# Linear attention with a routed MLP on one core: diagonals shared with ScalarE, products cut in quarters, two chunks' states in one product

## The chip, the core and the metric

The kernel runs on one core of one Trainium2 chip. The metric is device time in microseconds for one launch. The core has five engines with queues of their own: TensorE (PE) multiplies matrices, VectorE (DVE) and GpSimd (POOL) work element by element, ScalarE (ACT) copies and applies functions, and SyncE (SP) starts most of the loads. An engine works through its queue in order; an instruction that waits for a semaphore holds up all behind it.

## The reference

Two blocks follow each other. The first is a linear attention with decay: for every batch (4), head (8) and channel a state of 48 x 48 runs over 768 tokens.

```python
for t in range(S):
    kt, vt, rt = (k[:, :, t], v[:, :, t], r[:, :, t])
    cur = np.einsum('bhd,bhe->bhde', u[None] * kt, vt)
    y[:, :, t] = np.einsum('bhd,bhde->bhe', rt, state + cur)
    state = w[None, :, :, None] * state + np.einsum('bhd,bhe->bhde', kt, vt)
```

Its output, with the heads side by side, is x of shape (4, 768, 384). The second block gives every token a score `x @ w_gate`, takes the 128 best tokens of each batch, and adds to these rows `sigmoid(score) * (relu(x @ w1) @ w2)`, with 1024 hidden channels. All data are float32.

## The kernel before

**Units.** The tokens are cut into units of 128; unit n is part n % 6 of batch n // 6, 24 in all. A unit consists of two chunks of 64 tokens, c = 0 and 1. The eight heads are four pairs hp of an even and an odd head (i = 0, 1); the even head of a pair stands on partitions 0 to 47, the odd one on 64 to 111. The recurrence becomes products of matrices:

- `scaled` (L239) multiplies the keys by a table of decays, on POOL.
- `bonus` (L243) and `bonus_scaled` (L249) form r*k and r*k*u on POOL; `bonus_sum` (L253, DVE) adds them up to `du`, one number per token and head. `diagonal` (L257, POOL) spreads `du` over a diagonal: `at`, 128 partitions x 8 heads x 64.
- `turn` (L266, L271) transposes keys and r on PE; ScalarE copies the keys to `kh` (L276), DVE multiplies r by a table into `rh` (L281).
- `products` (L288) is k^T v: for each pair and head one product over all 128 tokens, with 48 weight columns and 96 moving columns. The values lie in `vpad` in blocks, so that columns 0 to 47 belong to chunk 0 and 48 to 95 to chunk 1. The result goes to `rp` in PSUM.
- `scores` (L298) is k r^T for each chunk and head, `masked` (L303, DVE) puts the causal half of it over the diagonal in `at`.
- `added` (L309, DVE) adds the product of a chunk to the state before it. For chunk 0 this gives the state between the chunks; for chunk 1 it gives the state after the unit, which ScalarE scales by the decay (L316, `z`, four activations).
- `states` (L328) multiplies r with the state before each chunk, `values` (L344) multiplies `at` with the values. Both add up in two PSUM banks, y0 for even heads and y1 for odd ones. Between the two stands a `mark`: a tiny copy on ScalarE (L332) that waits for the last products of `states`, and for which the first product of `values` waits.
- `finish` (L361, L363) copies y0 and y1 to x on ScalarE in three copies; `stored` writes x to memory, `score` (L378, DVE) forms the router's scores.

**Order.** The order is written out by hand, unit by unit; nothing is rearranged. In unit n, PE does states(n-1), products(n), scores(n), values(n-1), turn(n+1). ScalarE does mark(n-1), the copies of y of unit n-1, kh(n+1), z(n+1), and `along` (below). DVE does added(n, 0), masked(n), added(n, 1), rh(n+1), du(n+1), score(n-1) and router work. POOL does scaled(n+2), diagonal(n+1), bonus(n+2). The loads of unit n+4 (k, r and two halves of v) are started by SP one by one, each behind a DVE instruction of unit n; the weights follow in eight parts from unit 6 on.

**Router and MLP.** Extra work is hung on places in the units by `step(n, where, ...)` and done by `work_at(n, where)`. From unit 2 on, `scores_along` (L388, L390) turns a column of scores into a row on PE and ScalarE, and `compare` (L398, L400) counts on DVE how many are higher. Three units after a batch's last one, `pick` (L448 on PE, L452 and L455 on DVE) yields the indices of the chosen tokens, and `fetch` (L464) starts an indirect gather from POOL. `chosen` (L480, L482) transposes the rows to `xt`; the MLP is eight parts `hidden` (L491) and eight `expert` (L500), spread over six units. Where the parts go is in two lists, `MOVE0` for batch 0 and `MOVE` for the others. The MLP of the last batch stands behind all units.

```python
MOVE0 = (-1, -1, 0, 0, 0, 0, 1, 1, 2, 2, 3, 3, 4, 4, 5, 5)
step(n + 5 - (b == 0), "turn" if b == 0 else "scores", chosen, b, z)
step(n + 5 + (MOVE if b else MOVE0)[i * 16 // len(parts)], "end", f, *a)
```

Of the kernel before, what the change touches and what calls it, by code (L numbers as in the profile page):

```python
# [7 lines left out]
F32 = mybir.dt.float32  # L8
# [9 lines left out]
def kernel(  # L18
# [23 lines left out]
    nc = tc.nc  # L42
# [50 lines left out]
    def load(n, part=None, behind=None):  # L93


        b, c = divmod(n, NC)
        rows = slice(c * T, (c + 1) * T)
        if part is None:
            for part in range(4):
                load(n, part)  # L100
            return
        if n >= NU:
            return
        if part == 0:
# [130 lines left out]

    KH, RH, RK, RKU, DU, AT, ZA, ZB, YP = ({} for _ in range(9))

    def scaled(n):
        nc.gpsimd.tensor_mul(kws[n % 3][:, :, :D], KIN[n], wk)  # L239

    def bonus(n):
        rk = RK[n] = work.tile([128, H, D], F32, name="rk")
        nc.gpsimd.tensor_mul(rk, rpads[n % NIN][:, :, :D], KIN[n])  # L243
        if n:
            bonus_scaled(n, nc.gpsimd)

    def bonus_scaled(n, engine):
        RKU[n] = work.tile([128, H, D], F32, name="rku")
        engine.tensor_mul(RKU[n], RK[n], ub)  # L249
# [4 lines left out]

    def diagonal(n):
        AT[n] = work.tile([128, H, C], F32, name="at", bufs=3)
        nc.gpsimd.tensor_mul(AT[n], dia[:, None, :].to_broadcast([128, H, C]),  # L257
                             DU[n].rearrange("t i p -> t (i p)")[:, :, None].to_broadcast([128, H, C]))

    def turn(n, keys=None, between=None):  # L260
        def two_heads(x, hp):
# [18 lines left out]
    def turned(n, pr):  # L280
        return nc.vector.tensor_mul(RH[n][:CH], pr[:CH], tr[:CH])  # L281

    def products(n):

        for hp in range(NP):
            for i in range(2):
                at = NP * C + hp % 2 * 2 * D
                nc.tensor.matmul(out=rp[i * PAD : i * PAD + D, hp // 2, at : at + 2 * D],  # L288
                                 lhsT=kws[n % 3][:, 2 * hp + i, :D], rhs=VIN[n][:, 2 * hp + i, :],
                                 start=True, stop=True)  # L290

    def scores(n):
        for hp in range(NP):
# [7 lines left out]
    def masked(n):  # L301
        at = AT[n].rearrange("s (i p) t -> s i p t", i=2)
        return nc.vector.copy_predicated(at, causal, rp[:, :, : NP * C].rearrange("s i (p t) -> s i p t", p=NP))  # L303

    def added(n, c):
        z = ZA[n] if c == 0 else ZB[n]
        g = work.tile([128, NP, D], F32, name=f"g{c}", bufs=3)
        sums = rp[:, :, NP * C : NP * (C + D)].rearrange("d b (p e) -> d b p e", p=2)
        op = nc.vector.tensor_add(g.rearrange("d (b p) e -> d b p e", p=2), sums[:, :, :, c * D : (c + 1) * D],  # L309
                                  z.rearrange("d (b p) e -> d b p e", p=2))  # L310
        if c == 0:
            ZB[n] = g
            return op
        ZA[n + 1] = work.tile([128, NP, D], F32, name="z", bufs=3)
        for hp in range(NP):
            nc.scalar.activation(ZA[n + 1][:, hp, :], g[:, hp, :], AF.Copy, scale=wc[:, hp : hp + 1])  # L316

    def states(n):


        YP[n] = [psum.tile([128, 512], F32, name=x) for x in ("y0", "y1")]
        for hp in range(NP):
            for j in range(2):
                for i in range(2):
                    rows = slice(i * PAD, i * PAD + D)
                    c = j ^ i
                    z = ZA[n] if c == 0 else ZB[n]
                    mm = nc.tensor.matmul(out=YP[n][i][j * C : (j + 1) * C, hp * D : (hp + 1) * D],  # L328
                                          lhsT=RH[n][rows, hp, c * C : (c + 1) * C], rhs=z[rows, hp, :],
                                          start=(hp == 0), stop=False, skip_group_check=True)  # L330
                    END[i, j] = mm
        behind = nc.scalar.copy(mark, tr[:1, 0, :1])  # L332
        for mm in END.values():
            tc.add_manual_dep(behind.ins, mm.ins.name, wait_for, reason="a mark behind the states' part")
        return behind

    def values(n, behind):

        for hp in range(NP):
            for i in range(2):  # L340
                for j in range(2):
                    c = j ^ i
                    ts = slice(c * C, (c + 1) * C)
                    mm = nc.tensor.matmul(out=YP[n][i][j * C : (j + 1) * C, hp * D : (hp + 1) * D],  # L344
                                          lhsT=AT[n][ts, i * NP + hp, :],
                                          rhs=VIN[n][ts, 2 * hp + i, c * D : (c + 1) * D],
                                          start=False, stop=(hp == NP - 1), skip_group_check=True)
                    if hp == 0 and i == 0 and j == 0:
                        tc.add_manual_dep(mm.ins, behind.ins.name, wait_for,
                                          reason="y's banks: the other row half is done")  # L350
# [5 lines left out]
    def finish(n):  # L356
        b, c = divmod(n, NC)
        x = xa[b][:, c, :]
        to = x.rearrange("t (p i d) -> t i p d", p=NP, i=2)
        y = [YP[n][i][:, : NP * D].rearrange("t (p d) -> t p d", p=NP) for i in range(2)]  # L360
        nc.scalar.copy(to[:, 0], y[0])  # L361
        for j in range(2):
            nc.scalar.copy(to[(1 - j) * C : (2 - j) * C, 1], y[1][j * C : (j + 1) * C])  # L363

# [157 lines left out]

    fill = {}

    def step(n, where, f, *a):
        fill.setdefault((n, where), []).append((f, a))
# [5 lines left out]
            yield expert, (b, z, f)  # L534


    MOVE0 = (-1, -1, 0, 0, 0, 0, 1, 1, 2, 2, 3, 3, 4, 4, 5, 5)
    MOVE = (0, 0, 0, 0, 1, 1, 2, 2, 3, 3, 3, 4, 4, 4, 5, 5)

    def plan(b):  # L540
        n = (b + 1) * NC
        for j in range(NC):
            step(n - NC + j + 2, "turn", scores_along, b, j)
            step(n - NC + j + 2, "turn", compare, b, j)
        step(n + 1, "turn", count, b)
        step(n + 1, "turn", parts_of_scores, b)
        step(n + 2, "turn", rank, b)
        for z in range(NST):
            step(n + 2, "turn", match, b, z)
            step(n + 3, "scores", pick, b, z)  # L550
            step(n + 3, "scores", fetch, b, z)
            step(n + 5 - (b == 0), "turn" if b == 0 else "scores", chosen, b, z)
        parts = [p for z in range(NST) for p in mlp(b, z)]
        for i, (f, a) in enumerate(parts):
            step(n + 5 + (MOVE if b else MOVE0)[i * 16 // len(parts)], "end", f, *a)

    for b in range(B):
        plan(b)
# [1 line left out]
    def work_at(n, where):  # L560
        for f, a in fill.get((n, where), []):
            f(*a)
# [8 lines left out]
    nc.sync.dma_start(out=wg, in_=bass.AP(tensor=moe_w_gate.tensor, offset=moe_w_gate.offset, ap=[[0, 128], [1, Dm]]))  # L571
    load(3)
    turned(0, pr)
    bonus_scaled(0, nc.vector)
    bonus_sum(0)
    onward = const.tile([128, 128], F32)
# [1 line left out]
    ones = const.tile([128, 2], BF16)  # L578
    nc.vector.memset(ones[:, 0:1], 1.0)
    nc.vector.memset(ones[:, 1:2], 0.0)  # L580
    scaled(0)
    diagonal(0)
    scaled(1)
    bonus(1)
    for n in range(NU):
        if n == 2:
            late_tables()
        b, c = divmod(n, NC)
        if c == 0:
            ZA[n] = zt  # L590
        if n:
            behind = states(n - 1)
        products(n)
        scores(n)
        work_at(n, "scores")
        load(n + 4, 0, added(n, 0))
        op = masked(n)
        load(n + 4, 2, op)
        if n:
            values(n - 1, behind)  # L600
            finish(n - 1)
# [94 lines left out]
```

## Time and profile before

| | |
|---|---|
| median of 3 runs | 167.73 us (166.64 to 168.81) |
| profiled execution | 163.72 us |
| its span, first to last instruction | 161.9 us |
| busy: PE, DVE, ACT, POOL | 144.7, 111.3, 76.2, 117.5 us |
| granted TensorE clock | 1.00 |

The profiled execution is 1.8 us longer than its span, and 4.0 us shorter than the median of the runs. All stamps below are microseconds from the start of the span. A row of a timeline has start, duration, engine and line of the kernel, operation, output <- inputs, shapes and count; in brackets stands how long the engine sat idle before it, and what ended that. A float32 product shows as two matmul records, each with a weight load of its own. "issue" is idle time for which the profile finds no semaphore.

### The profile page before, as it was taken

How to read it: one execution, taken by the hardware profiler on the slowest of the kernel's cores; microseconds unless marked ns; L12 is line 12 of the kernel's file. 1: busy time of each engine (PE TensorE's matmuls, PEld its weight loads, DVE VectorE, ACT ScalarE, POOL GpSimd, SP SyncE). 2: the span in 40 equal slices, each digit the busy share in tenths (PEclk: the TensorE clock that was granted, in tenths of full speed). 3: DMA queues.
4: the chain of work that ended last, by engine and by line, in shares of the span. 5: the costliest groups of instructions: out<-in, count | busy, mean ns of one | idle time of the engine just before them, and what ended most of it. 6: DMA issues, size and time to landing. Idle time of an engine off the chain costs nothing.

```text
span 161.9 us, 7852 instructions
## 1 busy us (share of the span) xinstructions
PE 144.7 (89%) x3278; PEld 118.3 (73%) x3278; DVE 111.3 (69%) x352; ACT 76.2 (47%) x251; POOL 117.5 (73%) x156
## 2 busy tenths in 40 slices
PE   6969979678887959999999999999999999989970
PEld 2558858567776849999767879999696788748730
DVE  7856768899899975757999787488976956701010
ACT  6636655545454770555465444546606645102100
POOL 8699999999989999558899989688987421022002
PEclk9999999999999999999999999999999999999999
DMA  4998699999889989999999978786403112011001
GB/s 70 214 175 158 146 221 201 197 195 202 173 192 215 242 205 208 237 227 220 208 260 225 225 152 211 178 183 148 103 4 101 55 49 101 0 49 53 0 0 49
DMA packets 82659, 24.50 MB, mean 151 GB/s; under 512 B 76352, under 2 KB 82240, under 8 KB 82624
## 3 DMA queue, kind: packets, MB, share of 16 engines
q1 hardware_dynamic: 79888, 19.67, 57.4%
q10 hardware_dynamic: 2224, 2.75, 4.8%
q0 software_dynamic: 512, 1.57, 2.7%
q8 instruction: 26, 0.43, 1.1%
q14 instruction: 9, 0.07, 0.2%
HBM read 18.48 MB, written 5.51 MB: 148 GB/s over the span
## 4 chain that ended last, share of the span: by engine, by line
PE 59%; POOL 16%; issue 12%; DMA 6%; DVE 2%; ACT 1%; POOLq 1%; ACTq 0%
PE m L491 10%; PE rp L288 8%; PE m L500 7%; PE rp L298 6%; PE y L328 6%; PE m L266 6%; PE y L344 5%; PE m L271 4%; POOL kw L239 4%; POOL at L257 4%; POOL rk L243 4%; DMA kin<-in_k_dram 3%; DMA xr<-out_dram,idx 3%; POOL rku L249 3%; PE m L138 3%
## 5 line engine op out<-in xcount | busy, mean ns | idle before, releaser
L257 POOL TENSOR_TENSOR at<-dia,du 128x512 f32<-128x512 f32 x24 | 29.7, 1237 | 10.9 <-DVE du L253 10.9
L288 PE MATMUL rp<-vpad,kw 128*48 128x96 f32 x384 | 21.2, 251 | 4.5 <-issue 1.7
L249 POOL TENSOR_TENSOR rku<-rk,ub 128x384 f32<-128x384 f32 x23 | 23.1, 1005 | 1.8
L239 POOL TENSOR_TENSOR kw<-kin,wk 128x384 f32<-128x384 f32 x23 | 23.8, 1035 | 0.3 <-DMA kin<-in_k_dram 0.2
L491 PE MATMUL m<-xt,w 128*128 128x128 f32 x192 | 23.3, 277 | 0.5 <-ACT xt L482 0.5
L491 PEld LDWEIGHTS m<-xt,w 128*128 128x128 f32 x192 | 22.3, 192 | 1.3 <-ACT xt L482 1.2
L243 POOL TENSOR_TENSOR rk<-rpad,kin 128x384 f32<-128x384 f32 x23 | 23.0, 999 | 0.0
L500 PE MATMUL m<-w,ht 128*128 128x384 f32 x64 | 22.7, 490 | 0.1
L361 ACT COPY x<-y 128x192 f32<-128x192 f32 x24 | 7.6, 319 | 31.4 <-PE y L344 29.1
L316 ACT ACTIVATE z<-g,wp 128x48 f32<-128x48 f32 x80 | 20.2, 326 | 1.9 <-DVE g L309 1.8
L288 PEld LDWEIGHTS rp<-vpad,kw 128*48 128x48 f32 x384 | 16.3, 122 | 6.5 <-issue 3.0
L281 DVE TENSOR_TENSOR rh<-m,tables 112x512 f32<-112x512 f32 x24 | 16.5, 688 | 5.2 <-PE m L271 3.3
L328 PE MATMUL y<-g,rh 48*64 48x48 f32 x384 | 17.1, 223 | 2.6 <-issue 2.6
L303 DVE COPY_PREDICATED at<-mask,rp 128x512 f32<-128x512 uint32 x24 | 17.7, 736 | 2.4 <-POOL at L257 2.4
L378 DVE SCALAR_TENSOR_TENSOR scr<-x,wg 128x384 f32<-128x384 f32 x24 | 17.0, 707 | 1.8 <-ACT x L363 1.8
L328 PEld LDWEIGHTS y<-z,rh 48*64 48x64 f32 x320 | 12.2, 134 | 7.0 <-issue 4.7
L298 PE MATMUL rp<-rh,kh 48*64 48x64 f32 x768 | 16.7, 224 | 0.0
L400 DVE TENSOR_SCALAR_CACHE_REDUCE gt<-along,sc 128x128 bf16<-128x128 f32 (+5 forms) x24 | 16.2, 675 | 0.2 <-issue 0.2
L266 PE MATMUL m<-ident,kw 128*112 128x128 f32 x92 | 14.9, 285 | 1.1 <-POOL kw L239 1.1
L298 PEld LDWEIGHTS rp<-rh,kh 48*64 48x64 f32 x768 | 13.4, 134 | 3.2
L344 PE MATMUL y<-vpad,at 64*64 64x48 f32 x768 | 15.5, 218 | 0.2 <-ACT mark L332 0.2
L500 PEld LDWEIGHTS m<-w,ht 128*128 128x128 f32 x64 | 11.4, 191 | 5.9 <-ACT kh L276 0.3
(95 smaller groups left out, 251.3 us busy)
## 6 DMA issues: line engine op xcount, KB each, us to landing
rpad<-in_r_dram SPq DMA_DIRECT2D x24, 192.0 KB, 4.5
vpad<-in_v_dram SPq DMA_DIRECT2D x48, 96.0 KB, 4.4
kin<-in_k_dram SPq DMA_DIRECT2D x23, 192.0 KB, 4.1
w<-in_moe_w_dram SPq DMA_DIRECT2D x8, 384.0 KB, 5.5
out_dram<-x ACTq DMA_DIRECT2D x14, 192.0 KB, 3.9
out_dram<-x SPq DMA_DIRECT2D x10, 192.0 KB, 2.1
k<-in_k_dram SPq DMA_DIRECT2D x1, 192.0 KB
ub<-in_u_dram SPq DMA_DIRECT2D x1, 192.0 KB
```

What stands on the lines that cost most here:

```text
L239: nc.gpsimd.tensor_mul(kws[n % 3][:, :, :D], KIN[n], wk)
L243: nc.gpsimd.tensor_mul(rk, rpads[n % NIN][:, :, :D], KIN[n])
L249: engine.tensor_mul(RKU[n], RK[n], ub)
L257: nc.gpsimd.tensor_mul(AT[n], dia[:, None, :].to_broadcast([128, H, C]), DU[n].rearrange("t i p -> t (i p)")[:, :, None].to_broadcast([128 ...
L266: nc.tensor.transpose(pk[:CH, hp, :], two_heads(kws[n % 3] if keys is None else keys, hp), ident)
L288: nc.tensor.matmul(out=rp[i * PAD : i * PAD + D, hp // 2, at : at + 2 * D], lhsT=kws[n % 3][:, 2 * hp + i, :D], rhs=VIN[n][:, 2 * hp + i, ...
L298: nc.tensor.matmul(out=rp[ts, i, hp * C : (hp + 1) * C], lhsT=KH[n][rows, hp, ts], rhs=RH[n][rows, hp, ts], start=True, stop=True)
L316: nc.scalar.activation(ZA[n + 1][:, hp, :], g[:, hp, :], AF.Copy, scale=wc[:, hp : hp + 1])
L328: mm = nc.tensor.matmul(out=YP[n][i][j * C : (j + 1) * C, hp * D : (hp + 1) * D], lhsT=RH[n][rows, hp, c * C : (c + 1) * C], rhs=z[rows, h ...
L344: mm = nc.tensor.matmul(out=YP[n][i][j * C : (j + 1) * C, hp * D : (hp + 1) * D], lhsT=AT[n][ts, i * NP + hp, :], rhs=VIN[n][ts, 2 * hp + ...
L491: nc.tensor.matmul(out=ph[:, f % 4, :], lhsT=w1[:, d, f * 128 : (f + 1) * 128], rhs=XT[b, z][:, d, :], start=(d == 0), stop=(d == KD - 1))
L500: nc.tensor.matmul(out=pe[:, :Dm], lhsT=HT[b, z][:, f, :], rhs=w2[:, f, :], start=(f == 0), stop=(f == FB - 1))
```

## The change

1. `diagonal`: in units 1 to 10, POOL does four of the eight heads only; the others are four activations (copy with a scale from `du`) on ScalarE, behind z(n+1) in its queue. Unit 0 and units 11 to 23 stay on POOL.
2. `scaled(0)` moves from POOL to DVE.
3. For units 10, 16 and 22 `bonus_scaled` stands behind the gather of the unit before in POOL's queue, not ahead of it (`picking`).
4. `products` of units 15, 16, 17, 21, 22, 23 are cut in two by chunks (`quarters`): 64 tokens, 48 weight columns, 48 moving columns. There are 16 products instead of 8, chunk 0 in the first PSUM bank and chunk 1 in the second; `added` reads them there.
5. `states` of units 1 to 5 and 7 to 10 (`merged`): for even heads one product over all 128 tokens with both states side by side as 96 moving columns, instead of two of 64 tokens and 48 columns. Half of the result is not used. For this the two states of a unit share a tile (`states_of`), y0 gets 96 columns for each pair, and `finish` takes two copies of 64 partitions for even heads in these units, not one of 128.
6. In batch 0, `chosen` comes at the end of unit 10 (the router's transposes are ahead of it before and after), and the first two `hidden` parts come behind `states` in unit 11, not at the end of unit 10.

```diff
+    def scaled(n, engine=None):
+        (engine or nc.gpsimd).tensor_mul(kws[n % 3][:, :, :D], KIN[n], wk)
...
-        if n:
+        if n and not picking(n - 1):
             bonus_scaled(n, nc.gpsimd)
+    def picking(n):
+        return n % NC == 3 and n > NC
...
     def diagonal(n):
         AT[n] = work.tile([128, H, C], F32, name="at", bufs=3)
-        nc.gpsimd.tensor_mul(AT[n], dia[:, None, :].to_broadcast([128, H, C]),
-                             DU[n].rearrange("t i p -> t (i p)")[:, :, None].to_broadcast([128, H, C]))
+        du = DU[n].rearrange("t i p -> t (i p)")
+        own = H // 2 if 0 < n < 2 * NC - 1 else 0
+        nc.gpsimd.tensor_mul(AT[n][:, own:, :], dia[:, None, :].to_broadcast([128, H - own, C]),
+                             du[:, own:, None].to_broadcast([128, H - own, C]))
+        for h in range(own):
+            nc.scalar.activation(AT[n][:, h, :], dia, AF.Copy, scale=du[:, h : h + 1])
...
+    def quarters(n):
+        return n >= 2 * NC and n % NC >= NC // 2
...
+                h, to = 2 * hp + i, slice(i * PAD, i * PAD + D)
+                if quarters(n):
+                    for c in range(2):
+                        ts, at = slice(c * C, (c + 1) * C), NP * C + hp * D
+                        nc.tensor.matmul(out=rp[to, c, at : at + D], lhsT=kws[n % 3][ts, h, :D],
+                                         rhs=VIN[n][ts, h, c * D : (c + 1) * D], start=True, stop=True)
...
+    def merged(n):
+        return n % NC > 0 and n < 2 * NC - 1
+    def column(n, i, hp, c):
+        return (2 * hp + c) * D if i == 0 and merged(n) else hp * D
...
             for j in range(2):
-                for i in range(2):
+                if j == 0 and merged(n):
+                    END[0, 0] = END[0, 1] = nc.tensor.matmul(
+                        out=YP[n][0][:, column(n, 0, hp, 0) : column(n, 0, hp, 2)], lhsT=RH[n][:D, hp, :],
+                        rhs=ZZ[n][:D, hp].rearrange("d c e -> d (c e)"),
+                        start=(hp == 0), stop=False, skip_group_check=True)
+                for i in range(1 if merged(n) else 0, 2):
...
-        nc.scalar.copy(to[:, 0], y[0])
+        if merged(n):
+            both = YP[n][0][:, : 2 * NP * D].rearrange("t (p c d) -> t p c d", p=NP, c=2)
+            for c in range(2):
+                nc.scalar.copy(to[c * C : (c + 1) * C, 0], both[c * C : (c + 1) * C, :, c])
+        else:
+            nc.scalar.copy(to[:, 0], y[0])
...
-    MOVE0 = (-1, -1, 0, 0, 0, 0, 1, 1, 2, 2, 3, 3, 4, 4, 5, 5)
+    MOVE0 = (0, 0, 0, 0, 0, 0, 1, 1, 2, 2, 3, 3, 4, 4, 5, 5)
...
-            step(n + 5 - (b == 0), "turn" if b == 0 else "scores", chosen, b, z)
+            if b:
+                step(n + 5, "scores", chosen, b, z)
+            else:
+                step(n + 4, "end", chosen, b, z)
...
-            step(n + 5 + (MOVE if b else MOVE0)[i * 16 // len(parts)], "end", f, *a)
+            if b or i >= 2 * NST:
+                step(n + 5 + (MOVE if b else MOVE0)[i * 16 // len(parts)], "end", f, *a)
+            else:
+                step(n + 5, "states", f, *a)
...
+    scaled(0, nc.vector)
     bonus_scaled(0, nc.vector)
...
-    scaled(0)
+    scaled(1)
     diagonal(0)
-    scaled(1)
     bonus(1)
...
             behind = states(n - 1)
+        work_at(n, "states")
         products(n)
         scores(n)
         work_at(n, "scores")
+        if picking(n):
+            bonus_scaled(n + 1, nc.gpsimd)
```

More of the change, by code (lines that the diff above doesn't have):

```diff
@@ L236 @@
     KH, RH, RK, RKU, DU, AT, ZA, ZB, YP = ({} for _ in range(9))
-    def scaled(n):
-        nc.gpsimd.tensor_mul(kws[n % 3][:, :, :D], KIN[n], wk)
+    def scaled(n, engine=None):
+        (engine or nc.gpsimd).tensor_mul(kws[n % 3][:, :, :D], KIN[n], wk)
     def bonus(n):
@@ L286, in products @@
             for i in range(2):
[L287 to L290, printed above, removed]
+                h, to = 2 * hp + i, slice(i * PAD, i * PAD + D)
[5 more added lines that the diff above has]
+                else:
+                    at = NP * C + hp % 2 * 2 * D
+                    nc.tensor.matmul(out=rp[to, hp // 2, at : at + 2 * D], lhsT=kws[n % 3][:, h, :D],
+                                     rhs=VIN[n][:, h, :], start=True, stop=True)
     def scores(n):
@@ L303, in masked, with states_of @@
         return nc.vector.copy_predicated(at, causal, rp[:, :, : NP * C].rearrange("s i (p t) -> s i p t", p=NP))
+    ZZ = {}
+    def states_of(n):
+        if n not in ZZ:
+            ZZ[n] = work.tile([128, NP, 2, D], F32, name="z", bufs=3)
+        return ZZ[n]
     def added(n, c):
         z = ZA[n] if c == 0 else ZB[n]
[L307 to L310, printed above, removed]
+        if c == 0:
+            g = states_of(n)[:, :, 1, :]
+        else:
+            g = work.tile([128, NP, D], F32, name="g1", bufs=3)
+        sums = rp[:, :, NP * C : NP * (C + D)]
+        if quarters(n):
+            op = nc.vector.tensor_add(g, sums[:, c].rearrange("d (p e) -> d p e", p=NP), z)
+        else:
+            sums = sums.rearrange("d b (p e) -> d b p e", p=2)[:, :, :, c * D : (c + 1) * D]
+            op = nc.vector.tensor_add(g.rearrange("d (b p) e -> d b p e", p=2), sums,
+                                      z.rearrange("d (b p) e -> d b p e", p=2))
         if c == 0:
@@ L313, in added @@
             return op
-        ZA[n + 1] = work.tile([128, NP, D], F32, name="z", bufs=3)
+        ZA[n + 1] = states_of(n + 1)[:, :, 0, :]
         for hp in range(NP):
             nc.scalar.activation(ZA[n + 1][:, hp, :], g[:, hp, :], AF.Copy, scale=wc[:, hp : hp + 1])
+    def merged(n):
+        return n % NC > 0 and n < 2 * NC - 1
+    def column(n, i, hp, c):
+        return (2 * hp + c) * D if i == 0 and merged(n) else hp * D
     def states(n):
@@ L343, in values @@
                     ts = slice(c * C, (c + 1) * C)
-                    mm = nc.tensor.matmul(out=YP[n][i][j * C : (j + 1) * C, hp * D : (hp + 1) * D],
+                    at = column(n, i, hp, c)
+                    mm = nc.tensor.matmul(out=YP[n][i][j * C : (j + 1) * C, at : at + D],
                                           lhsT=AT[n][ts, i * NP + hp, :],
@@ L360, in finish @@
         y = [YP[n][i][:, : NP * D].rearrange("t (p d) -> t p d", p=NP) for i in range(2)]
-        nc.scalar.copy(to[:, 0], y[0])
+        if merged(n):
+            both = YP[n][0][:, : 2 * NP * D].rearrange("t (p c d) -> t p c d", p=NP, c=2)
+            for c in range(2):
+                nc.scalar.copy(to[c * C : (c + 1) * C, 0], both[c * C : (c + 1) * C, :, c])
+        else:
+            nc.scalar.copy(to[:, 0], y[0])
         for j in range(2):
@@ L551, in plan @@
             step(n + 3, "scores", fetch, b, z)
-            step(n + 5 - (b == 0), "turn" if b == 0 else "scores", chosen, b, z)
+            if b:
+                step(n + 5, "scores", chosen, b, z)
+            else:
+                step(n + 4, "end", chosen, b, z)
         parts = [p for z in range(NST) for p in mlp(b, z)]
         for i, (f, a) in enumerate(parts):
-            step(n + 5 + (MOVE if b else MOVE0)[i * 16 // len(parts)], "end", f, *a)
+            if b or i >= 2 * NST:
+                step(n + 5 + (MOVE if b else MOVE0)[i * 16 // len(parts)], "end", f, *a)
+            else:
+                step(n + 5, "states", f, *a)
     for b in range(B):
```

## The prediction

> **What bounds the kernel now.** I read the page first, then the chain, then the timelines of TensorE (PE), ScalarE (ACT) and GpSimd (POOL), the waits, and the DMA queues. From the page:
>
> ```profile
> PE 144.7 (89%) x3278; PEld 118.3 (73%) x3278; DVE 111.3 (69%) x352; ACT 76.2 (47%) x251; POOL 117.5 (73%) x156
> PE   6969979678887959999999999999999999989970
> DMA  4998699999889989999999978786403112011001
> PE 59%; POOL 16%; issue 12%; DMA 6%; DVE 2%; ACT 1%; POOLq 1%; ACTq 0%
> ```
>
> The row of digits shows two stages: up to slice 15 (some 60 us) PE has holes, after it none until the tail. The chain has the seam:
>
> ```profile
> 54.25 5.00 DMA xr<-out_dram,idx
> 59.39 0.53 PE m L480 x3
> 60.48 1.60 PE m L491 x12
> 62.69 0.80 PE rp L288 x16
> ```
>
> At 54.25 the first gather is issued, at 59.39 its rows are transposed, and from 60.48 PE is dense. So there are two prices: in the front, what delays products of unit 11 (62.69); after that, PE time itself. One dense unit of the chain:
>
> ```profile
> 73.33 0.61 PE y L328 x32
> 73.94 0.80 PE rp L288 x16
> 74.74 0.62 PE rp L298 x32
> 75.36 0.45 PE y L344 x32
> ```
>
> All of these but L288 run in quadrants of the array. 32 records in quadrants cost 0.45 us when the run before them was in quadrants too (L344 after L298), but 0.61 to 0.62 when another shape came before: a change of shape costs 0.16. L288 (two column halves, all rows, 96 columns) takes 0.80, of which 0.16 is its change: 0.08 for one pair of records.
>
> What paces the front? PE's timeline in units 7 and 8:
>
> ```profile
> 41.04 0.70 PE L288 MATMUL rp<-vpad,kw 128*48 128x96 f32 x12 [0.97 <-issue]
> 42.19 0.63 PE L344 MATMUL y<-vpad,at 64*64 64x48 f32 x32
> 45.72 0.54 PE L288 MATMUL rp<-vpad,kw 128*48 128x96 f32 x8 [0.68 <-issue]
> ```
>
> Once in each unit PE stands for 0.7 to 1.3 us with nothing named: resumptions at 31.04, 36.08, 41.04, 45.72, 50.42, 55.01. A unit has 121 matmul records with as many weight loads; the stalls lie 124 to 126 records apart, and the DMA page has 26 packets on the instruction queue. These are fetches of PE's program. PE's loop from L344 to L344 is, with the chain's durations, 0.45 (L344) + 0.58 + 0.44 (transposes) + 0.11 (L388) + 0.61 + 0.80 + 0.62 = 3.6 us, with the stall 4.5; seen are 4.8 (37.39 to 42.19) and 4.5. POOL is as full: no gap over 0.4 us from 6.07 to 59.87, four operations of 1.0 to 1.24 a unit, 4.3 together. But where POOL gets ahead, it meets the loads:
>
> ```profile
> 30.86 1.00 POOL L239 TENSOR_TENSOR kw<-kin,wk 128x384 f32<-128x384 f32 x1 [0.15 <-DMA kin<-in_k_dram]
> ```
>
> ScalarE looks idle (47%), but its queue is a chain of its own:
>
> ```profile
> 42.86 0.32 ACT L361 COPY x<-y 128x192 f32<-128x192 f32 x1 [2.07 <-PE y L344]
> 43.20 0.64 ACT L363 COPY x<-y 64x192 f32<-64x192 f32 x2
> 43.87 0.58 ACT L276 COPY kh<-m 112x512 f32<-112x512 f32 x1
> ...
> 44.35 1.01 ACT L316 ACTIVATE z<-g,wp 128x48 f32<-128x48 f32 x4
> 45.26 0.24 ACT L390 COPY along<-m 128x128 f32<-128x128 f32 x1
> 45.41 0.18 ACT L332 COPY mark<-tables 1x1 f32<-1x1 f32 x1
> 47.37 0.32 ACT L361 COPY x<-y 128x192 f32<-128x192 f32 x1 [1.78 <-PE y L344]
> ```
>
> The values product (L344) must wait for the mark, and the next copies of y for the values. From start to start: 0.34 + 0.67 + 0.48 + 0.91 + 0.15, mark 0.18, 0.13 until PE starts (134.09 to 134.22 in the chain), 0.67 until the next copy (46.70 to 47.37): 3.53 us at least, against 4.5 to 5.6 seen. This is the slack that the change spends.
>
> [...]
>
> **The change part by part.**
>
> Half of the diagonals on ScalarE, units 1 to 10. POOL's 1.24 us is halved; small POOL operations take 0.20 (the 128x6 subtractions), so I take 0.2 + 0.5 = 0.7: 0.5 saved. ScalarE gets four activations of 128x64; the nearest row is z, four of 128x48 at 0.91/4 = 0.23 start to start. I take 0.24: 0.96 a unit (bounds 0.9 and 1.1). They stand between z and along, so they delay the mark, on which PE's values wait, and the row of scores that DVE compares. They also wait for du.
>
> Copies of y in merged units: four of 64 partitions instead of one of 128 and two of 64: +0.33. ScalarE's loop becomes 3.53 + 0.96 + 0.33 = 4.8 us. In units 1 and 2, where it was 3.6 and 4.5, that is a loss at once.
>
> One product for both chunks, units 1 to 5 and 7 to 10. For each pair of heads two quadrant products become one of 64 rows x 128 columns with 96 moving columns; the odd head's two stay in quadrants. 32 records become 24, 16 instructions fewer to fetch. But the shape now changes twice for each pair. No row of before shows this change, which is only in columns and between different row halves. Lower bound: nothing drains and the odd head runs beside: 4 x 2 records x 0.08 = 0.64 us, about the 0.61 of now. Upper: 8 changes x 0.16 + 0.64 + 16 records x 0.014 (0.45/32) = 2.15 us. I take the upper, because every change seen costs that[...]: +1.55 us. PE's loop becomes 3.6 + 1.55 = 5.15 us, above ScalarE's 4.8; the stalls for fetching vanish within it, since 113 records in 5.15 us need a block only every 5.7.
>
> Start: scaled(0) goes to DVE, where 128x384 takes 0.55 (L249 there) against 1.91 on POOL. The first products start at 8.3 instead of 9.12. But values(0) now stands behind diag(1), which needs du(1): rku(1) ends near 12.9 on POOL, whose kw(1) waits for the load, du 13.45, four activations 14.5, mark: 14.8 instead of 14.01. So nothing is gained.
>
> Rku of units 10, 16, 22 behind the gather: on POOL the gather is no longer held up by 1.0 us; du(10) comes later, which ScalarE's diag(10) feels by less than 0.3. In the new front the gather is not late: PE arrives after the rows.
>
> Hidden parts 0 and 1 moved behind states(10): the xt copy (0.49) is covered by states. Same work, taken as zero.
>
> Quarters, units 15 to 17 and 21 to 23. L288 becomes 32 quadrant records: 0.45, with no change of shape before or after it. L288 and L298 took 0.80 + 0.62 = 1.42; they would take 0.90, and I count 0.45 of the 0.52. Six units: 2.7. In unit 15 the pick at 85.97 follows DVE's last oh (85.8), so there only 0.1 is saved; 32 more instructions a unit also bring fetches nearer in 15 to 17, where DMA is full. I take 2.0 (bounds 1.0 and 2.8).
>
> Sum. Values of units 0 to 9 were at 14.0, 17.6, 22.1, 27.0, 32.6, 37.4, 42.2, 46.7, 52.3, 56.6. After: 14.8, then 8 x 5.15, 4.8 for values(6) (states not merged), and 0.6 for rank and pick: values(9) at 61.4. Then values, transposes and L388 (1.6), chosen 0.5, states(10) 2.15, two hidden parts 1.5: products(11) at 67.2 instead of 62.69, +4.5. With -2.0 for the quarters: +2.5 us on the profiled 163.72, so 166.2. The median of the runs shown is 167.73, 4.0 above the profiled execution; I add the difference to it: 170.2.
>
> **Rivals.** Changes of shape cheap: products on different row halves may overlap. Then ScalarE's 4.8 sets the front: values(9) near 58.1, xt at 62.1, products(11) at 63.6, +0.9, minus 2.0: 166.6. For it: quadrants of different rows do run together. Against: 0.16 in every other change.
>
> Faster: POOL is the front's true pace, and its relief counts. From the load-bound kw at 30.86 on, the gather comes 4 x 0.5 + 1.0 = 3.0 us earlier; with the quarters -5.0: 162.7. For it: POOL without gaps, at the gather's head. It decides only if ScalarE's loop stays under 4.3, that is, if activations and copies add less than 0.8 instead of 1.3 and shapes cost nothing.
>
> The quarters don't do what they are for: block fetches eat them in 15 to 17 and DVE the rest. Then +4.5 or more: 172.2 to 174.
>
> **How the numbers follow.** Changes of shape dear: 0.66 with the quarters working, own range 168.2 to 172.7. Cheap: 0.20. Faster: 0.05. Quarters lost: 0.09. A difference of 2% (3.35 us, about what a measurement can tell) begins at 171.1: the first case passes it with 0.25 of its 0.66, the last with 0.09; of the cheap case 0.01 falls below 164.4. So slower 0.34, faster 0.06, within 0.60. The range leaves out the faster case, the cheap one's lower part and the worst of the lost quarters: 165.8 to 173.0.
>
> **What would show it.** Right: states rows (even heads) of 2 us in merged units, the values 5.15 apart, ScalarE with 0.96 of at in each unit and its wait for y below 1, no unnamed stall in the front, products(11) near 67; in units 16 and 22 products and scores 0.9 together. Wrong, first of all, if the merged states take 0.7 us; then the spacing of values is 4.8 with ScalarE never waiting. If it is below 4.5, my ScalarE loop is mis-sized.

## The result, and the profile after

The changed kernel takes 183.75 us (median; 181.42 to 184.52), the kernel before 167.19 us in the same sessions: ratio 1.098 [1.069, 1.128]. Ratios here and below compare the faster executions of the two kernels, with a 95% interval. The forecast was 170.2 us with a range of 165.8 to 173.0. It gave a slower kernel a chance of 0.34, but the loss is more than six times the 2.5 us that it forecast. The profiled execution took 184.46 us with a span of 182.7, against 163.72 and 161.9 before: 20.8 us more by the traces, 16.6 by the medians.

The page of the changed kernel, the same rows as those shown of before, and one that was not shown there because it was all nines, the granted clock of TensorE:

```profile
PE 170.9 (94%) x3302; PEld 140.3 (77%) x3302; DVE 115.1 (63%) x353; ACT 89.1 (49%) x300; POOL 110.6 (61%) x155
PE   7996999999999999999999999879999999999990
PEclk9999786786789966786999999999999999999998
DMA  5998987464555879387477999694881312101101
```

TensorE went from 144.7 to 170.9 us of busy time with only 24 more records, GpSimd and VectorE became less busy as a share, and DMA left its nines in the front. That is not a stage in which another engine or a load took over; TensorE itself became slow. The third row says in part why: from slice 5 to slice 19 (18 to 87 us) the clock is 0.6 to 0.8 in most slices.

The seam and the first dense unit in the chain of waits (before: 59.39 chosen, 62.69 products of unit 11, then 0.61, 0.80, 0.62, 0.45):

```profile
78.65 0.40 PE m L535 x3
81.60 2.38 PE m L546 x12
83.97 1.45 PE rp L309 x16
90.35 0.61 PE y L377 x32
90.97 0.80 PE rp L309 x16
```

Products of unit 11 start 21.3 us later. Twelve records of hidden cost 2.38 us here and 1.60 before, the products 1.45 instead of 0.80, and once past 85 us the dense unit has exactly its old prices. So all of the loss lies ahead of unit 12.

One merged unit of the front, on TensorE's timeline (start, length, group of records):

```profile
38.07 0.46 PE L369 MATMUL y<-z,rh 48*128 48x96 f32 x2
38.46 0.32 PE L377 MATMUL y<-z,rh 48*64 48x48 f32 x4
...
39.98 0.46 PE L369 MATMUL y<-z,rh 48*128 48x96 f32 x2
40.37 0.32 PE L377 MATMUL y<-z,rh 48*64 48x48 f32 x4
40.62 1.09 PE L309 MATMUL rp<-vpad,kw 128*48 128x96 f32 x16
...
42.55 1.05 PE L394 MATMUL y<-vpad,at 64*64 64x48 f32 x32
43.53 1.10 PE L275 MATMUL m<-ident,kw 128*112 128x128 f32 x4
```

The states' part takes 2.55 us (38.07 to 40.62) at full clock instead of 0.61; the forecast took 2.15. Where a record of another shape follows, TensorE loses time that the profile shows as busy, 0.15 us a change by the runs below. "Drain" in the recorded texts is a name for this lost time; what TensorE does in it is not shown. What follows, from 41.12 on, runs at half clock: from group to group the values take 0.98 instead of 0.56 us, the transposes of k 0.89 instead of 0.49. No stall stands in this unit, as forecast. (That the stalls of before are fetches of PE's program is the forecast's reading of two of its numbers: 26 packets on the instruction queue for 3278 records, one for every 126, and stalls 124 to 126 records apart. No run tries it.) The values are 7.26 to 7.57 us apart in the merged units with a halved stretch, instead of 4.5 to 5.6 before; where the clock was full all the way they are 5.51 (unit 0 to 1) and 5.59 (6 to 7). ScalarE waits for TensorE, although its own loop grew:

```profile
36.37 0.64 ACT L414 COPY x<-y 64x192 f32<-64x192 f32 x2 [2.50 <-PE y L394]
39.25 1.07 ACT L267 ACTIVATE at<-dia,du 128x64 f32<-128x64 f32 x4
43.63 0.64 ACT L414 COPY x<-y 64x192 f32<-64x192 f32 x2 [2.71 <-PE y L394]
```

Of the 7.26 us from copy to copy, 2.71 are this wait, with the rest of ScalarE's queue behind it, and 0.27 one for TensorE ahead of the mark. The other 4.28 and the 0.8 that lie between mark and copy (0.13 + 0.67 in the forecast) make 5.1 us, a little more than my 4.8 and less than TensorE's turn: ScalarE does not set the pace.

The clock is worth its own view. The trace lists it with its changes: 1.00 or 0.50, nothing between, in stretches of 3.413 us or a multiple, but for the one that ends the trace (3.622). One such length is called a window below. Halved stretches begin at 20.64, 27.47, 34.30, 41.12, 47.95, 65.02 (6.83 long), 75.26 and 82.08, and one more in the tail. Cut at that grid (columns: stretch, sum, then busy time and instructions of PE, PEld, DVE, ACT, POOL, clock, DMA share, GB/s):

```profile
17.23:20.64 3.41, 3.41 (x70) 2.78 (x73) 1.32 (x4) 2.31 (x10) 2.99 (x4) 1.00 1.04 231
20.64:24.06 3.42, 3.42 (x58) 3.00 (x51) 1.60 (x4) 2.18 (x7) 2.00 (x7) 0.50 0.80 153
24.06:27.47 3.41, 3.41 (x52) 2.69 (x56) 1.89 (x8) 1.97 (x9) 2.40 (x3) 1.00 0.89 203
27.47:30.88 3.41, 3.41 (x73) 3.20 (x65) 1.23 (x3) 1.71 (x5) 1.31 (x2) 0.50 0.75 142
```

The two stretches at full clock hold a states' part with its changes of shape, and the clock is halved right after each. From 24.06 on the full one does fewer records (52) than the halved one behind it (73). TensorE counts as busy in every microsecond of both kinds. What goes with the halving, on an engine that never shows as idle, the experiments below have to tell.

The kernel before is not free of this either: its trace is one of few executions at full clock. In the 56 executions of it that ran beside the experiments the granted clock is 0.957 to 1.00, with a median of 0.977, and the longer ones are mostly those with the lower clock. So part of the 4 us between its trace and its median is the clock's.

### The profile page after: what moved, and what is told of

Same layout as the page of the kernel before. It is cut to its first block, busy times and chain, and to the rows that moved or that the text cites. A ratio compares the mean times of both kernels' runs of the same rounds, so it can differ in the third digit from the quotient of the medians.

```text
span 182.7 us, 7959 instructions
## 1 busy us (share of the span) xinstructions
PE 170.9 (94%) x3302; PEld 140.3 (77%) x3302; DVE 115.1 (63%) x353; ACT 89.1 (49%) x300; POOL 110.6 (61%) x155
## 3 DMA queue, kind: packets, MB, share of 16 engines
HBM read 18.48 MB, written 5.51 MB: 131 GB/s over the span
## 4 chain that ended last, share of the span: by engine, by line
PE 71%; issue 9%; DVE 5%; POOL 5%; ACT 3%; DMA 2%; SPq 2%; POOLq 1%; DVEq 0%; ACTq 0%
PE m L546 9%; PE y L377 9%; PE y L369 8%; PE m L275 8%; PE y L394 8%; PE rp L309 8%; PE rp L318 7%; PE m L280 6%; PE m L555 5%; DVE scr L433 2%; DMA kin<-in_k_dram 2%; PE m L443 2%; SPq L114 1%; POOL at L264 1%; POOL rk L243 1%
## 5 line engine op out<-in xcount | busy, mean ns | idle before, releaser
L264 POOL TENSOR_TENSOR at<-dia,du 128x512 f32<-128x512 f32 (+1 forms) x24 | 24.3, 1011 | 35.5 <-DVE du L257 34.1
L546 PE MATMUL m<-xt,w 128*128 128x128 f32 x192 | 24.2, 283 | 0.0
L546 PEld LDWEIGHTS m<-xt,w 128*128 128x128 f32 x192 | 23.0, 197 | 0.6 <-ACT xt L537 0.5
L377 PE MATMUL y<-z,rh 48*64 48x48 f32 x560 | 21.8, 226 | 0.0
L433 DVE SCALAR_TENSOR_TENSOR scr<-x,wg 128x384 f32<-128x384 f32 x24 | 21.4, 892 | 0.4 <-ACT x L418 0.4
L377 PEld LDWEIGHTS y<-z,rh 48*64 48x64 f32 x560 | 15.4, 134 | 7.7 <-issue 2.9
L394 PE MATMUL y<-vpad,at 64*64 64x48 f32 x768 | 18.5, 243 | 2.2 <-ACT mark L381 2.2
L394 PEld LDWEIGHTS y<-vpad,at 64*64 64x64 f32 x768 | 16.5, 160 | 3.0 <-POOL at L264 1.5
L309 PE MATMUL rp<-vpad,kw 128*48 128x96 f32 x288 | 17.6, 271 | 0.6 <-issue 0.4
L369 PE MATMUL y<-z,rh 48*128 48x96 f32 x72 | 16.9, 315 | 0.0
L414 ACT COPY x<-y 64x192 f32<-64x192 f32 x18 | 5.6, 313 | 22.7 <-PE y L394 22.6
L280 PE MATMUL m<-ident,rpad 128*112 128x128 f32 x96 | 16.6, 301 | 0.0
```

The source lines that it names most:

```text
L264: nc.gpsimd.tensor_mul(AT[n][:, own:, :], dia[:, None, :].to_broadcast([128, H - own, C]), du[:, own:, None].to_broadcast([128, H - own, C]))
L280: nc.tensor.transpose(pr[:CH, hp, :], two_heads(rpads[n % NIN], hp), ident)
L309: nc.tensor.matmul(out=rp[to, hp // 2, at : at + 2 * D], lhsT=kws[n % 3][:, h, :D], rhs=VIN[n][:, h, :], start=True, stop=True)
L369: END[0, 0] = END[0, 1] = nc.tensor.matmul(out=YP[n][0][:, column(n, 0, hp, 0) : column(n, 0, hp, 2)], lhsT=RH[n][:D, hp, :], rhs=ZZ[n][:D ...
L394: mm = nc.tensor.matmul(out=YP[n][i][j * C : (j + 1) * C, at : at + D], lhsT=AT[n][ts, i * NP + hp, :], rhs=VIN[n][ts, 2 * hp + i, c * D : ...
L433: return nc.vector.scalar_tensor_tensor(scr, xa[b][:, c, :], 1.0, wg, op0=OP.mult, op1=OP.mult, accum_out=sc[b][:, c : c + 1])
```

## The experiments

Theory A: the alternation of shapes in the merged states' part costs it all, by the time lost at each change and by the clock. Theory B: ScalarE's added diagonals and copies cost it. Theory C: a stream on TensorE without holes lowers the clock whatever its shapes. Diffs are against the changed kernel where it says nothing else; those with sentences in place of code are shortened.

### Nothing merged, the rest of the change kept

```diff
     def merged(n):
-        return n % NC > 0 and n < 2 * NC - 1
+        return False
```

> The changed kernel with every product of states kept in quadrants (nothing merged; the diagonals on ScalarE, the quarters and the moves stay). Theory A, the alternation of shapes in the states' part costs it all: states back to about 0.61 us, granted clock 1.00 throughout, values 4.5 to 4.8 us apart, quarters still saving about 1.2 us: 163 to 168 us. Theory B, the added work of ScalarE's loop costs it: still 175 us or more, values more than 5.5 us apart. Theory C, a TensorE stream without holes lowers the clock whatever its shapes: clock still below 0.95 and more than 172 us.

Measured: 164.45 us (before 165.51; ratio 0.999 [0.994, 1.004]), clock 0.986 in the profiled execution, states 0.68 us from first start to last end (as in before), values of units 1 to 7 4.4 to 4.7 us apart. Theory B falls: ScalarE does its four activations in units 1 to 10, and the time is that of before. The spacing fits my 3.53 + 0.96 = 4.5. Theory C falls as well, with one remainder: the clock is not full throughout, there is one halved window at 62.88, of which more below. This kernel keeps the quarters, which alone bring a ratio of 0.982 (below), and yet stands at 0.999: the diagonals and the moves together take back about what the quarters save. The moves were not tried alone.

### The merge alone, put into the kernel before

```diff
-        own = H // 2 if 0 < n < 2 * NC - 1 else 0
+        own = 0
     def quarters(n):
-        return n >= 2 * NC and n % NC >= NC // 2
+        return False
```

and the moves of `scaled`, `bonus_scaled`, `chosen` and `hidden` taken back.

> The kernel before with the merged products of units 1 to 5 and 7 to 10 alone (diagonals on GpSimd, no quarters, nothing moved). Theory A: 184 to 189 us, states 2.55 us in a merged unit at full clock, granted clock about 0.91 over the span. Theory B: no more than 172 us, since only 0.33 us of copies is added on ScalarE. Theory C: between, with the clock as low as the front has no holes.

Measured: 183.67 us, just under the range of theory A, ratio 1.119 [1.102, 1.136], clock 0.923, states 2.62 us from first start to last end. The whole loss is in this part. The clock is full until 30.74 here, so that the first turns show the changes of shape without the clock. This is the stretch from values of unit 1 (20.11) to those of unit 2 (25.66), with the columns of the table above:

```profile
20.11:25.66 5.55, 5.55 (x126) 4.60 (x122) 4.19 (x11) 3.08 (x11) 5.47 (x10) 1.00 0.85 179
```

TensorE's turn is 5.55 us, busy all the time and at full clock; before it was 4.47 between the same units.

### The same products in another order

```diff
-        for hp: merged product of the even head, two quadrant products of the odd head
+        for hp: merged product of the even head
+        for hp: two quadrant products of the odd head
```

> The changed kernel with the four merged products first and the eight quadrant products of the odd heads after them: two changes of shape in a unit instead of eight, the same records. If the changes of shape are the cause, of the drains and of the clock: states 0.7 to 1.0 us, clock 1.00, 163 to 169 us. If records of 64 rows by 128 columns themselves lower the clock: clock below 0.95 and 172 us or more.

Measured: 165.87 us, ratio 1.011 [0.995, 1.026], clock 0.998, no window halved before the tail. Time and clock are back, within the interval, with the same products of the same shapes; only their order differs. So the loss comes from the alternation; the merged product itself costs little here. The timeline of one unit prices the parts:

```profile
31.53 1.13 PE L367 MATMUL y<-z,rh 48*128 48x96 f32 x8
32.59 0.67 PE L377 MATMUL y<-z,rh 48*64 48x48 f32 x16
33.19 0.87 PE L309 MATMUL rp<-vpad,kw 128*48 128x96 f32 x16
```

Start to start: 1.06 for eight merged records (0.112 apart, and a change), 0.60 for sixteen of the odd heads (a pair every 0.058, and a change), 1.66 to the products. I had expected 0.7 to 1.0. The records alone are 8 x 0.112 + 8 x 0.058 = 1.36 us, against 0.45 for 32 records in four quadrants: the merged ones all sit in one half of the rows and follow each other, the odd heads use two quadrants of four.

### In groups of two

Two merged products, four quadrant products, and again: four changes of shape instead of eight.

```diff
+        for g in range(0, NP, 2):
+            for hp in (g, g + 1): merged product of the even head
+            for hp in (g, g + 1): two quadrant products of the odd head
```

> The changed kernel with the states' part in groups of two pairs: two merged products, four quadrant products, and again: four changes of shape inside the part's order instead of eight, the same records. If each change costs 0.15 us: states 2.0 us (2.62 with eight changes, 1.73 with two), TensorE's loop 5.0 us, values 5.0 to 5.1 us apart at full clock, clock 0.98 or more, 166 to 170 us. If any alternation inside the part halves the clock: clock 0.95 or less and 174 us or more.

Measured: 170.35 us, ratio 1.028 [1.012, 1.044]; clock 0.956 to 0.983, in two of four executions below the 0.98 that I gave; states 2.02 us from first start to last end, values 4.95 apart. With 1.73 (two changes), 2.02 (four) and 2.62 (eight), each change costs 0.15 us, twice over. One halved window, at 65.08. The ratios to the kernel before are 1.011, 1.028 and 1.098, and TensorE's turns at full clock 4.7 to 4.8, 4.95 and 5.55 us. In nine merged units the last step is 9 x 0.6 = 5.4 us of changes, but the ratio grows by 0.070, which is some 11.6 us of 166. The changes don't explain that; the clock, 0.91 to 0.93 with eight changes, is what else differs.

### Alternation of other shapes, nothing merged

Products and scores of the kernel before, pair of heads by pair of heads; the scores move into the loop of the products (diff against the kernel before):

```diff
+            scores(n, hp)
...
         products(n)
-        scores(n)
```

> The kernel before with products and scores issued pair of heads by pair of heads, in all 24 units: eight changes between column halves and quadrants instead of two, the same records, nothing merged. At 0.15 to 0.16 us a change: products and scores 2.3 to 2.4 us together instead of 1.42, a dense unit 5.8 us instead of 4.9, 176 to 180 us. The clock stays 1.00 if it follows the work done in a window[...]; below 0.95 and 185 us or more if any alternation halves it.

Measured: 180.04 us (two executions; ratio 1.086 [1.074, 1.098]), clock 0.987.

```profile
32.55 0.37 PE L288 MATMUL rp<-vpad,kw 128*48 128x96 f32 x4
32.86 0.34 PE L299 MATMUL rp<-rh,kh 48*64 48x64 f32 x8
33.13 0.37 PE L288 MATMUL rp<-vpad,kw 128*48 128x96 f32 x4
```

A pair takes 0.58, four pairs 2.3 instead of 1.42: six more changes, 0.15 each. So the price of a change is the same 0.15 between these shapes, and eight changes a unit did not halve the clock here: it is full but for one window at 63.47 and the tail.

### Slow without alternation

The reverse test: the kernel before, in its own shapes and order, held back by idle copies on ScalarE (diff against the kernel before).

```diff
+        for _ in range(6 if 0 < n < 2 * NC - 1 else 0):
+            nc.scalar.copy(scrap[:CH], tr[:CH])
         behind = nc.scalar.copy(mark, tr[:1, 0, :1])
```

> The kernel before with six copies of 112 x 512 to a tile that nobody reads put on ScalarE ahead of the mark of units 1 to 10 (0.58 us each, so 3.5 us a unit): TensorE does the same work in the same shapes, nothing merged or alternating, at a pace of about 7.0 us a unit, the pace of the changed kernel. If too little work of the array in a window of 3.41 us halves the clock: several such windows between 20 and 85 us, as in the changed kernel, mean clock 0.91 to 0.97. If the alternation of shapes halves it: clock 1.00. Either way 182 to 190 us, ten units at 7.0 instead of 4.7.

Measured: 190.62 us (two executions), ratio 1.145 [1.125, 1.166], values 7.2 to 7.8 us apart, and a clock of 0.899, lower than the changed kernel's; time and clock lie just outside what I had written.

```profile
PEclk9999657867996675679999999999999999999999
27.46:30.87 3.41, 1.90 (x71) 1.70 (x70) 1.32 (x5) 2.44 (x7) 2.90 (x3) 1.00 0.73 142
30.87:34.29 3.42, 3.42 (x54) 2.88 (x52) 2.34 (x8) 3.24 (x10) 1.16 (x1) 0.50 0.60 142
34.29:37.70 3.41, 1.21 (x65) 1.00 (x63) 1.27 (x5) 2.72 (x6) 2.98 (x4) 1.00 0.58 109
```

The same see-saw with nothing merged: the clock is halved without alternation here, and in the experiment ahead of it there was alternation without a halved front. One thing is unlike the changed kernel: TensorE stands idle here for part of the full windows (busy 1.21 of 3.41 us in the last row).

To see what the two have in common, I estimated TensorE's work. The estimate takes a record's rows x columns x moving columns as a share of those of a record of L546 (128 x 128 x 128) and gives it that share of the 0.126 us that L546 measures (24.2 us / 192); the bf16 fill of the next experiment has its own measured 0.215 us. The weights were summed in each window of 3.413 us, in the traces of all fourteen kernels of this study, from 9 to 150 us, and divided by the window's length. Of the windows at full clock, 33 were followed by a halved one: their estimated work was 0.21 to 0.41. In 21 of these TensorE shows as busy throughout. Some 490 were followed by a full one: 15 of these lay between 0.33 and 0.41, the others above. Below 0.33 every window of these traces, 19 in all, was followed by a halved one.

The kernel before has one window below 0.42 between 12 and 90 us (0.35); the changed kernel's seven before a halved one between 24 and 82 us have 0.29 to 0.35. This is an estimate read over runs that differ in many ways, not a separate test, and how the clock is set is not shown. But halved windows in fronts without the merge fit it too: the one at 62.88 with nothing merged (work before it 0.30), and one at 51.44 in the kernel with the quarters alone, whose front is that of before (0.22). TensorE was waiting in both.

### Work added

```diff
             behind = states(n - 1)
+            if merged(n - 1):
+                warm(3)
```

> The changed kernel with three idle products of 128 x 128 by 512 columns (zeros, results not used) behind the states' part of every merged unit: work added, shapes still alternating. If the clock is halved because too little of the array works in a window of 3.41 us: the fill[...] lifts it, clock above 0.97, values 6.2 us apart instead of 7.3, 174 to 179 us, faster than the changed kernel though it does more. If the alternation itself halves the clock: clock at or below 0.92, values 7.9 us apart or more, 189 us or more.

Measured: 182.47 us (180.25 to 187.16), clock 0.952 to 0.990 in four executions against 0.911 to 0.928 of the changed kernel; in the profiled one, the longest, the halved time in the front is 17.1 us instead of 30.7. Each fill took 0.75 us at full clock, 6.8 in nine units, and the kernel is not slower. The clock rose, as the first theory said, but above 0.97 in only two of the four executions, and the time met neither figure. The windows ahead of the halved ones have an estimated work of 0.33 to 0.36, within the 0.21 to 0.41 of the others; mostly every fourth window was halved instead of every second. A fill of this size is no remedy.

### The merge in two units

```diff
-        return n % NC > 0 and n < 2 * NC - 1
+        return n in (3, 8)
```

> The changed kernel with the merged product in units 3 and 8 only. By the drains alone each merged unit makes TensorE's loop 3.6 + 1.94 = 5.5 us against the 4.65 us at which ScalarE's loop paces the front: 0.9 us a unit, 166 to 167 us, with the clock at 1.00. If one merged unit is enough to have the clock halved for a window of 3.41 us: two such windows (mean clock near 0.96), up to 1.7 us more each, 168 to 170 us.

Measured: 166.74 us (164.62 to 171.10, too wide for a ratio), clock 0.967 to 1.00. In the profiled execution unit 3 left the clock full and unit 8 was followed by a halved window at 53.82 (work before it 0.34). Inconclusive on the size; why a halved window follows the one unit and not the other is not shown.

### Both heads merged

The odd heads' chunks merged in the same way, in the other half of the rows, their result in natural rows:

```diff
-                if j == 0 and merged(n): merged product of the even head
-                for i in range(1 if merged(n) else 0, 2): quadrant products
+                for i in range(2): merged product of head i
```

> The changed kernel with the odd heads merged as well (their chunks in natural rows, so that the values use two of the four quadrants): all products of states 64 rows by 128 columns, in both halves of the rows in turn, no change of shape inside. If the two row halves run beside each other: states 0.16 + 8 x 0.112 = 1.05 us. If not: 0.16 + 16 x 0.112 = 1.95 us. Values 0.63 to 1.1 us. Clock 0.98 or more, 164 to 169 us; below 0.95 only if this shape itself halves it.

Measured: 167.46 us (two executions), ratio 1.011 [0.994, 1.028], clock 0.999. Most records of the two row halves start within 0.01 us of each other, and pairs follow in 0.112: they do run beside each other. States take 1.14 to 1.36 us, the values 1.13 (two quadrants instead of four). No alternation, no halved window ahead of the tail, and still nothing to win over the 0.61 of quadrants.

### The other parts, alone

Half of the diagonals on ScalarE in the kernel before:

> The kernel before with half of the diagonals on ScalarE in units 1 to 10 alone. Theory A: 164 to 169 us, clock 1.00, GpSimd's row of at near 0.7 us in these units and ScalarE with 0.96 us of at. Theory B: 175 us or more, values 5.5 us apart or more. My sum of ScalarE's loop (3.53 + 0.96 = 4.5 us) lets it cost nothing against the 4.5 to 5.6 of before.

Measured: 165.46 us, ratio 1.012 [0.998, 1.027], clock 1.00 in the profiled execution. Nothing is gained by it. GpSimd's half takes 0.80 us in the mean (I took 0.7), and GpSimd now waits 4.3 us in all for `du` between 15 and 60 us, where it waited 0.4 before: it has slack, and the front is not shorter. But the same edit lengthens ScalarE's loop to 4.5 us, so what the relief of GpSimd alone would bring is not shown.

The quarters in the kernel before:

> The kernel before with the quarters in units 15 to 17 and 21 to 23 alone. The prediction's step: products and scores together 0.9 us instead of 1.42 in these units, 2.0 us saved in all (1.0 to 2.8): 163.5 us against 165.5 (ratio 0.988). If fetches and VectorE eat it: ratio 0.995 or more.

Measured: 162.99 us, ratio 0.982 [0.973, 0.991]. From products of unit 12 to the end 90.1 us instead of 93.0: 2.9 saved, a little over my upper bound. Of the parts that were tried alone this is the one that pays.

The quarters in all units from 12 on:

```diff
     def quarters(n):
-        return n >= 2 * NC and n % NC >= NC // 2
+        return n >= 2 * NC
```

> The kernel before with the quarters in all units from 12 on, 12 instead of the 6 of the quarters alone. If the 0.45 us of each dense unit counts there too: 2.0 to 2.7 us below the quarters alone (163.0), so 160 to 161.5 us, ratio 0.97. If VectorE's and GpSimd's work in the units 12 to 14 and 18 to 20 takes it back: 162.5 us or more.

Measured: 166.45 us, ratio 1.004 [0.997, 1.010]: a miss. The list of TensorE's waits from 69 to 140 us (total, times, longest) shows where:

```profile
PE y L394 <- issue: 3.5, 4, 1.3
```

TensorE stands four times ahead of or within the values, 1.3 us at the longest, with nothing named as the cause. From 69 to 88 us TensorE is busy 16.65 us instead of 18.70 with the quarters in six units, while DMA is at 0.84 of its engines. TensorE resumes from two of these stalls at 72.31 and 77.83 us, 125 records apart; the stalls in the front of before lie 124 to 126 apart. With sixteen more records a unit the same distance is reached sooner. That they are the same stalls is read from this likeness, not tried separately.

## Why the prediction was wrong

**The price of a change was forecast rightly, and as the likeliest case: changes of shape are dear.** A change costs 0.15 us (0.16 in the forecast), in the merged part and between products and scores alike. But the changes and the work between them make only some 6.6 of the 17.7 us that the front loses; most of the rest is the clock, which the forecast does not have.

**The first mis-sized term is the work between the changes.** The sum was 8 x 0.16 + 0.64 + 16 x 0.014 = 2.15 us. The eight merged records are 0.112 apart instead of 0.08. The 0.08 had been read from another shape, two column halves side by side; why a record of 128 columns takes longer is not shown. The odd heads' records, in two quadrants instead of four, cost 0.029 each instead of 0.014. 8 x 0.15 + 8 x 0.112 + 16 x 0.029 = 2.56, and 2.55 is seen. The loop is 5.55 us at full clock instead of 5.15.

**The step that failed is the silent one that every row keeps the duration it had in the trace of before.** Every price of the sum was taken at a clock of 1.00, and the forecast never said so. The runs show a clock of 0.91 to 0.93 in its place, halved for 30.7 us of the front.

From values of unit 0 (15.19) to those of unit 9 (75.49) the front takes 60.3 us. At full clock I estimate 8 x 5.55 + 4.8 for unit 6 = 49.2, so about 11 us are the clock's. The 5.55 is measured in the kernel with the merge alone. The estimate fits the 24 us of halved stretches inside the front: the values (0.98 instead of 0.56) and the transposes (0.89 instead of 0.49) take 1.8 times as long there, and 24 us at that rate cost some 10.5.

The sum of the 20.8 us is: start 1.2; front 60.3 - 42.6 = 17.7 (some 6.6 of it loop, 11.1 clock); values of unit 9 to products of unit 11 8.4 - 6.05 = 2.4, of which the states' part of unit 10 is 2.0; unit 11 0.7, still at half clock at its start; after unit 12 -1.2.

**"Stalls vanish" was right**, but nothing was won by it: the changes of shape (8 x 0.15 us a unit) took their place, on an engine that shows as 94% busy.

**ScalarE's loop** was right without the merge (4.5 us; 4.4 to 4.7 seen) and a little small with it (4.8; 5.1 by the trace). **GpSimd as the pace** was given 0.05; the diagonals alone gained nothing, which fits without settling it.

**The start:** values of unit 0 were given as 14.8 and begin at 15.19, the first products as 8.3 and begin at 9.00.

**Quarters:** 2.0 forecast, 2.9 alone, 1.2 in the changed kernel; products and scores together take 0.84 in units 16 and 22 (0.9 in the forecast). Units 21 to 23 and the tail save 1.9 in both, but units 15 to 17 take 18.0 us (before 17.1, quarters alone 16.3). With nothing merged they take 17.0, so part of this loss does not come from the merge; whether `bonus_scaled` behind the gather makes it was not tried apart.

**The rivals:** cheap changes would have had states of 0.7, and the lost quarters ended at 174. No case and no bound reached 183.75, since none of them let the other rows become slower.

## What to carry to other kernels

Fewer matmul instructions were not less TensorE time here: 24 records in two shapes by turns took 2.55 us at full clock, 32 in quadrants 0.61. Count what runs side by side before and after, add the price of a change (0.15 us here) for each change of shape in the order in which it is issued, and group by shape first: the same 24 records with two changes took 1.66 us. Then ask whether the durations that are added up still hold. All were read at a clock of 1.00, and some 11 of the 20.8 us lost are what that left out, by my estimate above. In a profile where PE is busier with about as many records (170.9 us for 3302 here, 144.7 for 3278 before), read the clock's row before the waits.

## What was not expected of the hardware

- The clock is halved while TensorE shows as busy without a gap (3.41 of 3.41 us at 17.23, 24.06 and 30.88). What goes with the halving in these traces is the estimated work, not the busy share: it was 0.21 to 0.41 in the 33 full windows ahead of a halved one, and TensorE was busy throughout in 21 of them.
- Of 41 halved windows in the fourteen traces, 33 were followed by a full one. In the merged units with a halved stretch the values stand 7.26 to 7.57 us apart, and two windows are 6.83 us; whether the loop falls into step with the clock is not shown.
- A merged product of 64 rows x 128 columns with 96 columns moving costs 0.112 us a record at full clock; two in different halves of the rows start within 0.01 us of each other, and the pairs follow in the same 0.112.
